# Seven products in another order: splitting A22·T4 a second time and computing (A12 − S2)·R22 last

## The chip, the cores and the metric

The kernel runs on one core of one Trainium2 chip. That core has five engines with instruction queues of their own: TensorE (PE in the profile; its weight loads are listed apart as PEld), VectorE (DVE), ScalarE (ACT), GpSimd (POOL) and SyncE (SP). In this kernel every engine's instructions run in the order in which the program writes them; semaphores hold an instruction back until what it needs is there. The metric is the device time of one execution in microseconds. The kernel before takes 731.65 us, the median of three runs (731.50 to 731.73).

## The reference, cut to what matters

Two branches work on the same x of 2048 rows by 1024 columns (bf16) and are mixed by a gate for each row:

```
g = sigmoid((x * gate_w).sum(-1, keepdims=True))
a = A(x)                       # q, k, v = x @ wqkv; 32 heads; each row looks at itself and
                               # 7 earlier rows, 2 apart; softmax; o @ wo
h = gelu(x @ w_gate) * (x @ w_up)          # 2048 x 3584
b = h @ w_down
return g * a + (1 - g) * b
```

The last step, o·wo and h·w_down together, is one product of 2048 rows, 4608 columns of inputs (3584 of h scaled by 1 − g, 1024 of o, into which g is already worked) and 1024 columns of output. This step is what the change touches.

## The kernel before, in words

Until about 512 us the kernel computes the gate, q, k and v, the attention and the two projections to h. The h and o that come out are stored to memory and loaded back in tiles as they are needed. The rest of the span, about 217 us, is the last product, and the function `down(s)` writes it for one half of the rows: `down(0)` for rows 0 to 1023, `down(1)` (in which `last` is true) for the others.

**First level.** For each half the product is cut into two by two by two blocks and computed with seven products in place of eight (Strassen's method in Winograd's form). A11, A12, A21, A22 are the blocks of the inputs; R11 to R22 those of the two weights; each block holds 18 tiles of 128 × 512 in bf16 (2304 KB). T1 to T4 are sums of R blocks, formed earlier and kept in memory (`t_d`). S = A21 + A22, AD = A11 − A21, and S2 = A22 − AD is written over A21. I number the products:

| product | operands | product | operands |
|---|---|---|---|
| 1 | A11 · R11 | 5 | S · T1 |
| 2 | A12 · R21 | 6 | S2 · T2 |
| 3 | (A12 − S2) · R22 | 7 | AD · T3 |
| 4 | A22 · T4 | | |

The four blocks of the output are 1 + 2; 1 + 6 + 5 + 3; 1 + 6 + 7 + 4 (T4 carries the sign); and 1 + 6 + 5 + 7. Two buffers in fp32 hold partial sums: `u2` holds product 1, then 1 + 6, then 1 + 6 + 7; `qs` holds product 5, then 1 + 6 + 5.

**A whole product** (`mm`, line 1049) is 72 matmuls of 128 × 512: four row tiles j, 18 tiles deep. **A split product** (`level2`, matmuls on line 1024) applies the same method a second time: seven sub-products of 18 matmuls of 128 × 256, so 126 in all. The sub-products run in a fixed order: two on untouched quarters of the operands, three on the sums number 0, 1 and 2, one on the left sum 3, one on the right sum 2. VectorE makes the sums: `forms_L` (line 985) and `forms_R` (line 993) have four instructions each, and the third of `forms_R` changes a quarter of the operand in place. ScalarE copies partial results from one part of PSUM to another between the sub-products (line 1029): after the first sub-product each of its two results is copied on, and the second sub-product adds onto the very place that is copied. Two more VectorE instructions (`joins`, line 1013) add the part that was kept aside, one after the sixth sub-product, one after the seventh.

**Banks.** The eight PSUM banks are dealt into two sets of four, XT (seen as XP) and VT (seen as VP). A split product adds onto what is in its banks, so ScalarE first zeroes the left halves of the set (`zero_left`, line 1005, two instructions for a set). The right halves are begun by ScalarE's copies.

**What sets the order.** `manual_schedule` takes each engine's instructions in program order. Ahead of `down` a small planner deals VectorE's background work into slots by a priority and a wake time; `run_last` finishes what is left of it, among it the scaling by 1 − g of blocks of half 0 (`scale_task`, line 906; pieces of four tiles). Inside `down` the order is written by hand: `take(rest, k)` issues k VectorE instructions from a prepared list, `run` all that are left. Sums over whole blocks are `comb_task` (line 913; five pieces). Results leave by `add_out` (line 1058, then a store on line 1054, which GpSimd's queue issues, or SyncE's for the last four). Loads (`loads`, lines 814, 816, 829, 832) go out on SyncE's queue in program order. Ten buffers of 18 KB in each partition hold blocks and sums; `plan` says for each half which name lies in which buffer, and a load into a buffer waits until its former content has been read.

**Before, half 0:** product 1 whole, 2 whole, 5 split (VT), 6 split (XT), 3 whole onto product 5 in VT, 7 split (XT), 4 whole (VT). **Half 1** is the same, with product 1 split too. In `down(0)` the sums for product 1 of half 1 are made after the sums for product 7. The step A12 − S2 lies ahead of product 6's right sums in half 0 (three of its five pieces), behind them in half 1. `mid6` is what is issued within product 6: joins of product 5, four ScalarE copies of it into `qs`, the loads of R22, T3 and T4.

The functions that the diff touches, and those that call them:

Of the kernel before, what the change touches and what calls it, by code (L numbers as in the profile page):

```python
# [9 lines left out]
ALU = mybir.AluOpType  # L10
# [5 lines left out]
P = 128  # L16
SC = 512
# [51 lines left out]
def kernel(  # L69
# [12 lines left out]
    nc = tc.nc  # L82
    Bsz, S, D = A_x.shape
# [51 lines left out]
    with tc.manual_schedule(engines={mybir.EngineType.PE, mybir.EngineType.DVE, mybir.EngineType.Activation,  # L135
# [296 lines left out]
        def bg(gen, prio, wake):  # L432
            t = Task(gen, prio, wake)
            tasks.append(t)
            tasks.sort(key=lambda t_: t_.prio)
            return t
# [437 lines left out]
        def tf_close():  # L874
            while tf_q[0] < N1:
# [5 lines left out]
        at_end(TFE - 1, tf_close)  # L881

        plan = [dict(A11=4, R11=5, A12=2, R21=7, A21=6, A22=3, T1=1, T2=9, S=8, AD=0, L5=4, R5=5, L6=7, R6=1,
                     R22=4, T3=8, T4=5, L7=7, R7=1),
                dict(A11=6, R11=9, L1=2, R1=4, A12=0, R21=7, A21=8, A22=1, T1=5, T2=4, S=6, AD=3, L5=9, R5=2, L6=7, R6=5,
                     R22=9, T3=6, T4=2, L7=7, R7=5)]
        u2 = regf(R_U2, 4 * SC).rearrange("p (j n) -> p j n", j=4)
        qs = regf(R_QS, 4 * SC).rearrange("p (j n) -> p j n", j=4)
        on = [0]
# [8 lines left out]
        def Bs(s):  # L898
            return {k: bufs[v] for k, v in plan[s].items()}

        def scale_task(b, s, c, ia, ib):
            t0 = s * SUP + c * SC
            om = omgrep[:, t0:t0 + SC].rearrange("p (o s) -> p o s", o=1)
            for i0 in range(ia, ib, 4):
                i1 = min(i0 + 4, ib)
                TT(out=b[:, i0:i1, :], in0=b[:, i0:i1, :], in1=om.to_broadcast([P, i1 - i0, SC]), op=ALU.mult)
                yield 0.05 + 0.273 * (i1 - i0)

        def comb_task(o_, a, b, op, step=4):
            for i0 in range(0, NK, step):  # L910
                i1 = min(NK, i0 + step)
                f = lambda t_: flat(t_[:, i0:i1, :])
                TT(out=f(o_), in0=f(a), in1=f(b), op=op)  # L913
                yield 0.05 + 0.273 * (i1 - i0)

        def run(*gens):
            for g in gens:
                for _ in g:
                    pass

        def pieces(*gens):
            for g in gens:
                yield from g

        def take(g, k):
            for _ in range(k):
                if next(g, None) is None:
                    break
# [14 lines left out]
        def pre_down_2(s):  # L943
            pd["end"] = True
            load_A(Bs(s)["A22"], s, 1, 1, 0, NE_, False)
            for k, c in (("A12", 0), ("A22", 1)):
                bg(scale_task(Bs(s)[k], s, c, 0, NE_), 7, n)
            if now[0] >= NX0 + 3:
                pre_down_3(s)

# [37 lines left out]
        def forms_R(f, b):  # L988
            f = quads(f)
            q = lambda kh, h: quarter(b, kh, h)  # L990
            for o_, a, b_, op in ((f[:, 0], q(0, 1), q(0, 0), ALU.subtract), (f[:, 1], q(1, 1), f[:, 0], ALU.subtract),
                                  (q(0, 1), q(1, 1), q(0, 1), ALU.subtract), (f[:, 2], q(1, 0), f[:, 1], ALU.subtract)):
                TT(out=o_, in0=a, in1=b_, op=op)  # L993
                yield 1.3

        def woven(*gens):
            for cs in zip(*gens):
                yield from cs
# [12 lines left out]
        def joins(bk, rf):  # L1011
            for i in range(2):
                TT(out=two_banks(bk, i, 1), in0=two_banks(bk, i, 1), in1=part5(rf), op=ALU.add)  # L1013
# [26 lines left out]
        def down(s):  # L1040
            B = Bs(s)
            last = s == 1
            eng = nc.gpsimd
            base = s * SUP
            XT, VT = (6, 7, 0, 1), (2, 3, 4, 5)

            def mm(ps, L, R, j, start, q0=0, q1=NK):
                for q, i in list(enumerate(KORD))[q0:q1]:
                    nc.tensor.matmul(ps, lhsT=L[:, i, j * P:(j + 1) * P], rhs=R[:, i, :], start=(start and q == 0),  # L1049
                                     stop=(q == NK - 1), skip_group_check=not start)  # L1050

            def emit(ot, c, nh, j):
                r0 = base + c * SC + j * P
                (nc.sync if last and (c, nh) == (1, 0) else eng).dma_start(out=o2[r0:r0 + P, nh * SC:(nh + 1) * SC], in_=ot)  # L1054

            def add_out(ps, t_, c, nh, j):
                ot = out_tile()
                TT(out=ot, in0=ps, in1=t_, op=ALU.add)  # L1058
                emit(ot, c, nh, j)

            A11, A12, A21, A22, S, AD = (B[k] for k in ("A11", "A12", "A21", "A22", "S", "AD"))
            XP = [bank(XT[j]) for j in range(4)]
            VP = [bank(VT[j]) for j in range(4)]
            if last:
                run(scale_task(A12, s, 0, 0, NE_))
                level2(XT, A11, B["R11"], B["L1"], B["R1"])
                rest = comb_task(AD, A11, A21, ALU.subtract)
                run(scale_task(A21, s, 1, 0, NE_))
                take(rest, 3)
                joins(XT, B["R1"])  # L1070
                for j in range(4):
                    nc.scalar.copy(out=u2[:, j, :], in_=XP[j])
                run(rest)
                loads(s, "T2")
            else:
                for j in range(4):
                    mm(XP[j], A11, B["R11"], j, True, 0, NK - 2)
                    if j == 0:
                        yield
                for j in range(4):  # L1080
                    mm(XP[j], A11, B["R11"], j, True, NK - 2, NK)
                    nc.scalar.copy(out=u2[:, j, :], in_=XP[j])
                run(scale_task(A21, s, 1, KX, NE_), comb_task(S, A21, A22, ALU.add), comb_task(AD, A11, A21, ALU.subtract))
            zero_left(VT)
            if last:
                run(scale_task(A22, s, 1, 0, NE_), comb_task(S, A21, A22, ALU.add))
            for j in range(4):
                mm(XP[j], A12, B["R21"], j, False)
                ot = out_tile()
                nc.scalar.copy(out=ot, in_=XP[j])  # L1090
                emit(ot, 0, 0, j)
            zero_left(XT)
            run(woven(forms_L(B["L5"], S), forms_R(B["R5"], B["T1"])))
            run(comb_task(A21, A22, AD, ALU.subtract))
            S2 = A21
            level2(VT, S, B["T1"], B["L5"], B["R5"])
            run(forms_L(B["L6"], S2))
            rest = comb_task(A12, A12, S2, ALU.subtract)
            if not last:
                take(rest, 3)  # L1100
            run(forms_R(B["R6"], B["T2"]), rest)

            def mid6():
                joins(VT, B["R5"])
                for j in range(4):
                    nc.scalar.copy(out=qs[:, j, :], in_=VP[j])  # L1106
                loads(s, "R22", "T3", "T4")

            level2(XT, S2, B["T2"], B["L6"], B["R6"], mid6)
            if not last:  # L1110
                loads(1, "A11", "R11")
            joins(XT, B["R6"])
            for j in range(4):
                TT(out=u2[:, j, :], in0=XP[j], in1=u2[:, j, :], op=ALU.add)
                TT(out=qs[:, j, :], in0=qs[:, j, :], in1=u2[:, j, :], op=ALU.add)
            zero_left(XT)
            rest = woven(forms_L(B["L7"], AD), forms_R(B["R7"], B["T3"]))
            for j in range(4):
                mm(VP[j], A12, B["R22"], j, False)
                take(rest, 2)  # L1120
                add_out(VP[j], u2[:, j, :], 0, 1, j)
            run(rest)
            if not last:
                N = Bs(1)
                run(scale_task(N["A11"], 1, 0, 0, NE_))
                run(woven(forms_L(N["L1"], N["A11"]), forms_R(N["R1"], N["R11"])))
            level2(XT, AD, B["T3"], B["L7"], B["R7"])
            joins(XT, B["R7"])
            if not last:
                loads(1, "A12", "A21", "R21", "A22")  # L1130
            for j in range(4):
                add_out(XP[j], qs[:, j, :], 1, 1, j)
                TT(out=u2[:, j, :], in0=XP[j], in1=u2[:, j, :], op=ALU.add)
            if not last:
                zero_left(XT)
            for j in range(4):
                mm(VP[j], A22, B["T4"], j, True)
                add_out(VP[j], u2[:, j, :], 1, 0, j)
            if not last:
                loads(1, "T1")  # L1140

        n = len(units)
# [78 lines left out]
```

## Time and profile before

| | |
|---|---|
| median of three runs | 731.65 us |
| the profiled execution | 731.21 us |
| its span | 729.4 us |
| last end of a matmul | 725.96 us |
| matmuls of half 0 in `down`, first to the start of half 1 | 512.48 to 623.39 us |
| matmuls of half 1 | 623.39 to 725.96 us |
| busy over the span: TensorE, VectorE, ScalarE, GpSimd | 714.7, 655.1, 317.2, 114.7 us |

The times in the profile are microseconds from the span's start. A line of the timeline gives the start, the length, the engine, the line of the kernel, the operation, what it writes and reads, how many instructions are merged in it and, in brackets, how long the engine was idle before it and who ended that. TensorE's busy time counts matmuls whose ends are modelled. The start of one group and the start of the next are therefore the better measure of what a product takes.

### The profile page before, as it was taken

Reading aid. Unit: us, or ns where it says so; the run is one execution under the profiler, and the core shown is the slowest. Engines: PE = TensorE matmul, PEld = TensorE weight load, DVE = VectorE, ACT = ScalarE, POOL = GpSimd, SP = SyncE. Lnnn points to the kernel's source line nnn. Section 1 sums busy time; section 2 is a strip of 40 time slices with the busy share of each in tenths; the row PEclk is TensorE's granted clock in tenths of the full one; section 3 lists DMA queues with packets and bytes.
Section 4 is the critical chain, followed back from the end, with each engine's and each line's share of the span. In section 5 each row is a group of like instructions: output and inputs, shape, how many; then the busy total and the mean of one; then the engine's idle time right before and its main releaser. Section 6 shows DMA issues by size and latency. Waiting matters only on the chain. (4 is left out here: it accounts for less than half of the span.)

```text
span 729.4 us, 10330 instructions
## 1 busy us (share of the span) xinstructions
PE 714.7 (98%) x3883; PEld 393.0 (54%) x3945; DVE 655.1 (90%) x703; ACT 317.2 (43%) x570; POOL 114.7 (16%) x212
## 2 busy tenths in 40 slices
PE   8999999999999999999999999999998999999998
PEld 4466666655544444444444444444457666758573
DVE  3699999999999999999999999999599698799944
ACT  4554445444557665555555555555131211232210
POOL 1233445143201210000010000001110011110001
PEclk9999999999999999999999999999999899999999
DMA  9967644287274834443363836563975766965501
GB/s 279 279 184 224 206 140 154 78 283 268 98 213 136 284 118 146 137 154 113 120 203 115 276 118 224 133 234 100 364 315 179 271 229 211 380 276 199 199 22 58
DMA packets 112626, 140.78 MB, mean 193 GB/s; under 512 B 18832, under 2 KB 94768, under 8 KB 111552
## 3 DMA queue, kind: packets, MB, share of 16 engines
q1 hardware_dynamic: 98368, 98.38, 42.0%
q0 software_dynamic: 13920, 41.21, 15.7%
q8 instruction: 31, 0.51, 0.3%
q10 hardware_dynamic: 288, 0.52, 0.3%
q14 instruction: 19, 0.16, 0.1%
HBM read 98.01 MB, written 39.99 MB: 189 GB/s over the span
## 5 line engine op out<-in xcount | busy, mean ns | idle before, releaser
L364 PE MATMUL banks<-arena 128*128 128x512 bf16 x2136 | 472.1, 380 | 4.1 <-DVE arena L401 0.7
L364 PEld LDWEIGHTS <-arena 128*128 128x128 bf16 x2184 | 240.2, 111 | 235.6 <-issue 7.0
L1049 PE MATMUL banks<-arena 128*128 128x512 bf16 x492 | 109.3, 379 | 1.0 <-ACT arena L1106 0.4
L401 DVE TENSOR_TENSOR arena<-banks,arena 128x1024 bf16<-128x1024 f32 x78 | 95.2, 1220 | 13.0 <-PE banks L364 7.6
L1024 PE MATMUL banks<-arena 128*128 128x256 bf16 x882 | 100.3, 277 | 3.7 <-DVE arena L993 3.7
L387 ACT COPY arena<-banks 128x512 f32<-128x512 f32 x78 | 45.7, 586 | 130.8 <-PE banks L364 130.8
L1024 PEld LDWEIGHTS <-arena 128*128 128x128 bf16 x882 | 87.3, 99 | 16.8 <-issue 4.2
L1049 PEld LDWEIGHTS <-arena 128*128 128x128 bf16 x504 | 49.2, 98 | 59.1 <-issue 0.6
L372 ACT CAST arena<-banks 128x512 bf16<-128x512 f32 x102 | 59.6, 584 | 42.4 <-PE banks L364 42.4
L743 DVE TENSOR_TENSOR arena<-arena 128x2048 bf16<-128x2048 bf16 x64 | 77.0, 1219 | 0.5
L750 DVE TENSOR_TENSOR arena<-arena 128x2048 bf16<-128x2048 bf16 (+2 forms) x96 | 73.8, 775 | 1.0
L596 DVE TENSOR_TENSOR arena<-arena 128x2048 bf16<-128x2048 bf16 x64 | 74.6, 1218 | 0.1
L394 ACT COPY banks<-banks 128x512 f32<-128x512 f32 x78 | 44.5, 570 | 21.9 <-PE banks L364 20.1
L258 POOL DMA_DIRECT2D h_d<-arena x28 | 15.1, 541 | 242.0 <-DVE arena L252 213.1
L382 ACT COPY banks<-banks 128x512 f32<-128x512 f32 x78 | 45.0, 576 | 13.6 <-PE banks L364 12.1
L1054 POOL DMA_DIRECT2D out_dram<-arena x28 | 15.2, 541 | 179.8 <-DVE arena L1058 130.0
L913 DVE TENSOR_TENSOR arena<-arena 128x2048 bf16<-128x2048 bf16 (+1 forms) x40 | 41.9, 1110 | 0.0
L1029 ACT COPY banks<-banks 128x256 f32<-128x256 f32 x42 | 14.9, 356 | 57.2 <-PE banks L1024 57.0
L321 DVE TENSOR_TENSOR arena<-arena 128x1024 bf16<-128x1024 bf16 x60 | 38.6, 685 | 0.5
L252 DVE TENSOR_TENSOR arena<-arena 128x2048 bf16<-128x2048 bf16 x28 | 34.0, 1216 | 5.5 <-ACT arena L372 4.1
L370 ACT ACTIVATE arena<-banks 128x512 bf16<-128x512 f32 x54 | 32.2, 597 | 15.4 <-PE banks L364 15.4
L985 DVE TENSOR_TENSOR arena<-arena 128x2304 bf16<-128x2304 bf16 x28 | 37.5, 1352 | 0.5
(85 smaller groups left out, 434.1 us busy)
## 6 DMA issues: line engine op xcount, KB each, us to landing
arena<-t_d SPq DMA_DIRECT2D x8, 2304.0 KB, 12.5
h_d<-arena POOLq DMA_DIRECT2D x28, 512.0 KB, 3.6
arena<-in_B_w_down_dram SPq DMA_DIRECT2D x6, 1792.0 KB, 14.5
t_d<-arena POOLq DMA_DIRECT2D x36, 256.0 KB, 4.1
arena<-h_d SPq DMA_DIRECT2D x6, 1536.0 KB, 11.0
arena<-in_B_w_gate_dram SPq DMA_DIRECT2D x15, 512.0 KB, 5.2
arena<-in_B_w_up_dram SPq DMA_DIRECT2D x15, 512.0 KB, 4.6
arena<-in_B_w_down_dram SPq DMA_DIRECT2D x28, 256.0 KB, 7.0
```

Of the source, the lines that this page charges most:

```text
L364: self.pe = nc.tensor.matmul(ps, lhsT=self.L[form](kt), rhs=rhs[:, kt, :], start=(start and kt == 0), stop=(kt == HK - 1), skip_group_chec ...
L372: nc.scalar.copy(out=o_, in_=i_)
L382: nc.scalar.copy(out=self.Y, in_=self.X)
L387: nc.scalar.copy(out=self.p5s, in_=self.V)
L394: nc.scalar.copy(out=self.Z, in_=self.Y)
L401: TT(out=self.T[:, :, c2s], in0=pair, in1=self.p5s.rearrange("p (o n) -> p o n", o=1).to_broadcast([P, 2, SC]), op=ALU.add)
L596: TT(out=dst, in0=q.rearrange("p (o s) -> p o s", o=1).to_broadcast([P, NWIN, AC]), in1=_win_ap(k, [[-DIL, NWIN], [1, AC]]), op=ALU.mult)
L743: TT(out=prod2[(t // 2) % 2][:, t % 2], in0=ab, in1=_win_ap(v[:, t, HALO:HALO + AC], [[SJ, NJ], [-DIL, NWIN], [1, SJ]]), op=ALU.mult)
L750: TT(out=out_, in0=h(0), in1=h(1), op=ALU.add)
L913: TT(out=f(o_), in0=f(a), in1=f(b), op=op)
L1024: nc.tensor.matmul(c(i, h, j), lhsT=l[:, kt, j * P:(j + 1) * P], rhs=r[:, kt, :], start=False, stop=(kt == KH - 1), skip_group_check=True)
L1049: nc.tensor.matmul(ps, lhsT=L[:, i, j * P:(j + 1) * P], rhs=R[:, i, :], start=(start and q == 0), stop=(q == NK - 1), skip_group_check=not ...
```

## The change

Product 4 is split as well, in both halves, so that a half has one whole product fewer. Product 3 stays whole, but moves to the end of the half, into VT afresh, and no longer onto product 5; its block of the output comes from `qs` and no longer from `u2`. The sequence of a half is now 1, 2, 5, 6, 7 (in VT), 4 (in XT), 3 (in VT).

Around it: the joins of product 5 come ahead of the third right sum of product 6, and A12 − S2 behind all of product 6's sums in both halves. `mid6` zeroes VT for product 7 and loads T3 alone. T4 and R22 are loaded after product 6. Four of product 7's eight sums are issued ahead of the joins of product 6 and the additions into `u2`, four behind; then the additions into `qs`, then `zero_left(XT)` for product 4, then product 7. The loads of A11 and R11 for half 1 are issued after product 7 and no longer after product 6. In half 0 the scaling of A11 and the eight sums for product 1 of half 1 are dealt among the row tiles of product 3. The last stores, now those of product 3, go on SyncE's queue in half 1. In the work that is left over before `down(0)`, A22 is scaled ahead of the last piece of A12. The buffers are dealt anew.

```
-                     R22=4, T3=8, T4=5, L7=7, R7=1),
-                dict(A11=6, R11=9, L1=2, R1=4, A12=0, R21=7, A21=8, A22=1, T1=5, T2=4, S=6, AD=3, L5=9, R5=2, L6=7, R6=5,
-                     R22=9, T3=6, T4=2, L7=7, R7=5)]
+                     T3=8, L7=4, R7=5, T4=9, L4=1, R4=7, R22=6),
+                dict(A11=0, R11=4, L1=5, R1=8, A12=3, A21=9, R21=1, A22=7, T1=2, AD=6, S=0, T2=8, L5=4, R5=5, L6=1, R6=2,
+                     T3=0, L7=4, R7=5, T4=8, L4=2, R4=1, R22=9)]
...
-            for k, c in (("A12", 0), ("A22", 1)):
-                bg(scale_task(Bs(s)[k], s, c, 0, NE_), 7, n)
+            for k, c, ia, ib in (("A12", 0, 0, 8), ("A22", 1, 0, NE_), ("A12", 0, 8, NE_)):
+                bg(scale_task(Bs(s)[k], s, c, ia, ib), 7, n)
...
-                (nc.sync if last and (c, nh) == (1, 0) else eng).dma_start(out=o2[r0:r0 + P, nh * SC:(nh + 1) * SC], in_=ot)
+                (nc.sync if last and (c, nh) == (0, 1) else eng).dma_start(out=o2[r0:r0 + P, nh * SC:(nh + 1) * SC], in_=ot)
...
             run(forms_L(B["L6"], S2))
-            rest = comb_task(A12, A12, S2, ALU.subtract)
-            if not last:
-                take(rest, 3)
-            run(forms_R(B["R6"], B["T2"]), rest)
+            rest = forms_R(B["R6"], B["T2"])
+            take(rest, 2)
+            joins(VT, B["R5"])
+            run(rest, comb_task(A12, A12, S2, ALU.subtract))
 
             def mid6():
-                joins(VT, B["R5"])
                 for j in range(4):
                     nc.scalar.copy(out=qs[:, j, :], in_=VP[j])
-                loads(s, "R22", "T3", "T4")
+                zero_left(VT)
+                loads(s, "T3")
 
             level2(XT, S2, B["T2"], B["L6"], B["R6"], mid6)
-            if not last:
-                loads(1, "A11", "R11")
+            loads(s, "T4", "R22")
+            rest = woven(forms_L(B["L7"], AD), forms_R(B["R7"], B["T3"]))
+            take(rest, 4)
             joins(XT, B["R6"])
             for j in range(4):
                 TT(out=u2[:, j, :], in0=XP[j], in1=u2[:, j, :], op=ALU.add)
+            run(rest)
+            for j in range(4):
                 TT(out=qs[:, j, :], in0=qs[:, j, :], in1=u2[:, j, :], op=ALU.add)
             zero_left(XT)
-            rest = woven(forms_L(B["L7"], AD), forms_R(B["R7"], B["T3"]))
+            level2(VT, AD, B["T3"], B["L7"], B["R7"])
+            if not last:
+                loads(1, "A11", "R11")
+            run(woven(forms_L(B["L4"], A22), forms_R(B["R4"], B["T4"])))
+            joins(VT, B["R7"])
             for j in range(4):
-                mm(VP[j], A12, B["R22"], j, False)
-                take(rest, 2)
-                add_out(VP[j], u2[:, j, :], 0, 1, j)
-            run(rest)
-            if not last:
-                N = Bs(1)
-                run(scale_task(N["A11"], 1, 0, 0, NE_))
-                run(woven(forms_L(N["L1"], N["A11"]), forms_R(N["R1"], N["R11"])))
-            level2(XT, AD, B["T3"], B["L7"], B["R7"])
-            joins(XT, B["R7"])
+                add_out(VP[j], qs[:, j, :], 1, 1, j)
+                TT(out=u2[:, j, :], in0=VP[j], in1=u2[:, j, :], op=ALU.add)
+            level2(XT, A22, B["T4"], B["L4"], B["R4"])
+            joins(XT, B["R4"])
+            for j in range(4):
+                add_out(XP[j], u2[:, j, :], 1, 0, j)
             if not last:
                 loads(1, "A12", "A21", "R21", "A22")
+                zero_left(XT)
+                N = Bs(1)
+                rest = pieces(scale_task(N["A11"], 1, 0, 0, NE_), woven(forms_L(N["L1"], N["A11"]), forms_R(N["R1"], N["R11"])))
             for j in range(4):
-                add_out(XP[j], qs[:, j, :], 1, 1, j)
-                TT(out=u2[:, j, :], in0=XP[j], in1=u2[:, j, :], op=ALU.add)
+                mm(VP[j], A12, B["R22"], j, True)
+                if not last:
+                    take(rest, 3)
+                add_out(VP[j], qs[:, j, :], 0, 1, j)
             if not last:
-                zero_left(XT)
-            for j in range(4):
-                mm(VP[j], A22, B["T4"], j, True)
-                add_out(VP[j], u2[:, j, :], 1, 0, j)
-            if not last:
+                run(rest)
                 loads(1, "T1")
```

## The prediction

> **What bounds the kernel now.** I read the page first, then the table of the last product by stretches, the chain that ended last, and the timeline of half 0 around the places that the diff names.
>
> ```profile
> PE 714.7 (98%) x3883; PEld 393.0 (54%) x3945; DVE 655.1 (90%) x703; ACT 317.2 (43%) x570; POOL 114.7 (16%) x212
> ```
>
> TensorE is the bound over the whole span, and VectorE is close behind. So fewer matmuls help only where VectorE follows. The stretches of the last product (from:to, length, busy time and count of each engine, granted clock, DMA share, GB/s):
>
> ```profile
> 562.40:566.10 3.70, 0.03 (x2) 0.01 (x1) 3.63 (x4) 0.00 (x0) 0.00 (x0) 0.81 1.16 444
> 566.10:571.50 5.40, 5.40 (x26) 3.74 (x26) 5.36 (x5) 0.74 (x2) 0.00 (x0) 0.50 0.51 218
> 571.50:578.60 7.10, 7.10 (x67) 6.31 (x66) 2.18 (x4) 3.40 (x8) 0.00 (x0) 1.00 0.70 246
> 652.70:680.90 28.20, 27.86 (x253) 24.59 (x252) 27.90 (x26) 7.88 (x21) 0.54 (x1) 1.00 0.48 173
> ```
>
> The first two rows show TensorE stopped and then at half its clock for 5.4 us: the stop costs more than its own length. In the last row VectorE and TensorE are both full, so half 1 has no room for more VectorE work there. The chain agrees; it runs through VectorE's sums until product 3 of half 1 starts, and through TensorE from there to the end:
>
> ```profile
> 674.52 4.14 DVE arena L913 x4
> 679.67 0.62 DVE banks L1013
> 681.38 10.74 PE banks L1049 x49
> 696.65 13.75 PE banks L1024 x126
> ```
>
> In the timeline of half 0 two things matter: the wait in product 6, and when ScalarE's zeroing gets through.
>
> ```profile
> 566.08 12.64 PE L1024 MATMUL banks<-arena 128*128 128x256 bf16 x90 [3.67 <-DVE arena L993]
> ...
> 578.56 15.70 PE L1049 MATMUL banks<-arena 128*128 128x512 bf16 x70
> ...
> 581.60 0.60 ACT L1005 ACTIVATE banks<-omgrep 128x512 f32<-128x512 bf16 x1 [4.38 <-DVE arena L1114]
> ...
> 584.41 0.60 ACT L1005 ACTIVATE banks<-omgrep 128x512 f32<-128x512 bf16 x1 [2.21 <-DVE arena L1114]
> ...
> 594.10 13.92 PE L1024 MATMUL banks<-arena 128*128 128x256 bf16 x126
> ...
> 595.34 0.36 ACT L1029 COPY banks<-banks 128x256 f32<-128x256 f32 x1 [10.32 <-PE banks L1024]
> ```
>
> The zeroing (line 1005) waits for the additions into `u2` (line 1114), and ScalarE's next copy (line 1029) comes behind it. Today a whole product, which needs nothing of ScalarE, runs meanwhile, so this costs nothing.
>
> **Prices, all from this trace.** A whole product 15.5 us (578.56 to 594.10). A split product 13.75 (594.10 to 607.85), so one sub-product 1.965. A sum for a split product 1.27 (eight from 540.54 to 550.69). A scaling piece 1.14 (six in 6.8, from 624.20). A block sum of five pieces 5.2 to 5.3. Two joins 1.3. An addition out of PSUM 0.6. A ScalarE zeroing 0.6, a copy 0.36.
>
> **The change, part by part.**
>
> *Product 4 split:* 15.5 − 13.75 = 1.8 us of TensorE saved in each half. VectorE gets eight sums and two joins, 10.15 + 1.3 = 11.5 us in each half; whether they are hidden follows below.
>
> *A12 − S2 behind product 6's sums:* three pieces, 3.4 us, leave the way of product 6's right sums. The wait of 3.67 goes, and with it the half clock: 90 matmuls took 12.64 where 90 × 13.75 / 126 = 9.8 is their due, so 2.8. Together 6.5 us, in half 0 only. Next late would be the right sum 0, which I put below 3 us ahead of need.
>
> *A22 scaled ahead of A12's last piece:* VectorE waited 3.00 us for that piece (until 525.37), while A22's load, issued at 504.6 and 11.7 us under way, was there. Three pieces fill the wait, so VectorE runs 3.0 us earlier and starts the sums for product 5 at 537.5 (before, 540.54). T1 bounds it: its load landed 19.0 us after 518.5, at 537.5. The gain lies between 0 and 3.0; I take 3.0 because that load is needed by the second sum only.
>
> *Product 7 straight behind product 6:* here the change adds a wait. ScalarE's order is now: the zeroing of XT, then product 7's copies. The zeroing waits for `u2`, `u2` for the joins of product 6, and these for product 6's end. Product 7's second sub-product adds onto what the copy must first read, so TensorE can issue one sub-product and then stops. Even an idle VectorE leaves 1.3 + 2.45 + 1.2 + 0.4 = 5.3 us after product 6 against 1.965 of work. And VectorE isn't idle; half 0, in us from the span's start:
>
> VectorE: 537.5 + 10.15 (sums 5) + 5.3 (S2) + 5.1 (left sums 6) + 2.55 (two right sums) = 560.6, the right sum 0 being ready at 559.4; + 1.3 (joins) + 2.55 + 5.2 (A12 − S2) + 5.1 (four sums for 7) = 574.8; + 1.3 (joins of 6) + 2.45 (`u2`) = 578.5. TensorE: product 5 ends at 544.42 + 13.75 = 558.2, product 6 needs that right sum at 562.1 and ends at 572.0, one sub-product of product 7 ends at 573.95. Zeroing and copy let the second start at 579.7: a wait of 5.7. It is longer than the 3.67 that halved the clock, so I add that row's 2.8. The bounds are 0 and 3.4, half of the 6.8 us from the fall of the clock (a mean of 0.81 over 3.7 us means that its last 1.4 ran at half, so 564.7) to its return at 571.5. Product 7 ends at 579.7 + 11.8 + 2.8 = 594.3, product 4 at 608.05, product 3 at 623.6. Product 4's sums are done by 597, its third pair before need. Half 1 thus starts at 623.6, where it did (623.39): +0.2.
>
> [...]
>
> *Half 1, a chain of VectorE.* Its work from product 4's joins on (second join from 608.3 to 608.95): stores' additions 2.4, scaling A11 3.4, sums for product 1 10.15, product 3's additions 2.4, scaling A12 and A21 6.8, AD 5.2, joins 1.3, scaling A22 3.4, S 5.3, sums 5 10.15, S2 5.3, left sums 6 5.1, right sums 6 5.1, joins 1.3, A12 − S2 5.2, four sums 5.1, joins 1.3, `u2` 2.45: together 81.35, so 690.3. Nothing makes it wait: product 3's row tiles end at 611.9, 615.8, 619.7, 623.6, each before its addition is due. On the way the joins of product 1 start at 637.5 (three pieces of AD are ahead), while that product ends at 637.35; product 2 starts 1.4 us after the joins start (679.59 to 680.95 is that step before), at 638.9: a wait of 1.5. Products 2, 5 and 6 end at 654.4 and, with 27.9 for the pair as in 652.69 to 680.57, at 682.3. Product 7's first sub-product ends at 684.25, the zeroing and the copy at 691.5: a wait of 7.2, and 2.8 for the clock. Product 7 ends at 691.5 + 11.8 + 2.8 = 706.1, product 4 at 719.85, product 3 at 735.4. Before it was 725.96: +9.4 us.
>
> *Loads, queues, stores, at nothing each.* A11 and R11 of half 1 go out at 594.3 instead of 578.10; the longest landing of these kinds is 17.5 us, to 611.8, and A11 is scaled from 611.4, R11 used from 617: up to 0.4. The next four go out at 608.05 (607.39 before) and are used 2.7 us later than before. T3, issued at 558.5 without R22 ahead, lands 8.8 to 12.5 us later, by 571.0; its first use is at 572. T4, issued after product 6 at 572.0, lands by 584.5; its sum comes at 587.5. On SyncE's queue nothing else waits behind these. The number of stores is unchanged on each queue, and the tail from the last matmul to the span's end stays 3.44. If a load's cover is gone, VectorE's chain takes the excess one to one.
>
> **The sum.** Half 0: −1.8 − 6.5 + 5.7 + 2.8 = +0.2. Half 1: −1.8 − 0.4 (wait ahead of product 3 today) + 1.5 + 7.2 + 2.8 = +9.3. Together +9.5, by the chain +9.4. The profiled execution of 731.21 (span 729.4) becomes 740.6; the median is 0.44 above it, so 741.0.
>
> **Rivals.**
>
> *No hold on ScalarE (faster):* product 7's copies go through before the zeroing, or don't need it. Against it stands that the zeroing came before the copies in the trace, in program order. The point: the second zeroing must be over by 573.95, and it can't be before 576.9. Then product 7 waits only for its third pair of sums (1.2 in half 0). Half 0 ends at 616.3, `u2` in half 1 at 686.05, and TensorE at 688.6 + 5.9 + 13.75 + 15.5 = 723.8. That is −2.1: 729.5.
>
> *The hold without the clock:* both waits stay, the clock doesn't fall: 741.0 − 5.6 = 735.4. Against it: both are longer than the 3.67 that halved it.
>
> *VectorE doesn't get its 3 us, or a load or a finer wait holds it up by as much:* all of half 0's chain and with it half 1's shift: 744.0. For it: T1 lands on the very start of the sums. With 3.4 twice for the clock it would be 745.2.
>
> **How the numbers follow.** Two executions of this kernel differ by up to 0.23 us; 0.2%, 1.5 us, is what a measurement can tell from no change. The forecast (741, own range 738 to 743) has 0.70, VectorE later 0.15, the clock staying up 0.07, no hold 0.05, and 0.03 for a partial hold that ends within 0.2%. The range goes from 735.4 to 745.2. Faster 0.05, same 0.03, slower 0.92.
>
> **What would show it.** Right: zeroings of XT that wait for the additions into `u2` and stand just ahead of product 7's first copies; TensorE idle about 5.7 and 7.2 us inside product 7 with a ScalarE copy as releaser; the clock at 0.50 behind both; no wait in product 6 of half 0; half 1 starting at about 623.6; 1134 matmuls of 128 × 256 in the two halves. Wrong: no idle TensorE inside product 7, or a wait that VectorE's sums end. The step likeliest to be off is half 1's chain of 81 us on VectorE, in which 0.02 us an instruction already makes 1.4 us.

## The result, and the profile after

The changed kernel takes 742.94 us (median of four runs, 741.74 to 743.35) against 731.69 for the kernel before, measured beside it: a ratio of 1.0149, with a 95% interval from 1.0132 to 1.0167. It is 1.5% slower. The forecast was 741.0 with a range from 735.4 to 745.2. The profiled execution took 743.35 us, its span 741.6.

The page's line of engines (busy us, share of the span, instructions):

```profile
PE 719.0 (97%) x4053; PEld 406.4 (55%) x4053; DVE 676.6 (91%) x723; ACT 324.8 (44%) x590; POOL 115.1 (16%) x212
```

VectorE has 21.5 us more to do, near the 23 that the two splits add. TensorE is the bound in name only: it waits more than before (15.4 us in three stops, where before had 3.67 and 0.39), and part of its busy time is at half clock. The last product by stretches (from:to, length, busy time and count of PE, PEld, DVE, ACT, POOL, then granted clock, DMA share, GB/s):

```profile
574.70:582.20 7.50, 0.12 (x2) 0.05 (x1) 7.50 (x10) 1.57 (x4) 0.00 (x0) 0.86 1.02 384
582.20:587.50 5.30, 5.30 (x28) 3.77 (x28) 5.30 (x7) 0.17 (x1) 0.00 (x0) 0.55 0.58 183
...
639.30:641.90 2.60, 0.16 (x2) 0.00 (x0) 2.60 (x5) 0.61 (x2) 0.00 (x0) 0.93 1.13 429
641.90:645.00 3.10, 3.07 (x8) 1.12 (x8) 3.10 (x4) 2.46 (x5) 0.00 (x0) 0.51 1.02 433
...
688.70:694.30 5.60, 0.06 (x2) 0.03 (x1) 5.60 (x8) 1.55 (x4) 0.00 (x0) 0.86 0.98 390
694.30:700.00 5.70, 5.70 (x29) 4.00 (x29) 5.70 (x7) 0.20 (x1) 0.00 (x0) 0.54 0.88 280
```

Three stops of TensorE, each followed by a stretch at about half clock: in product 7 of half 0, ahead of product 2 of half 1, in product 7 of half 1. VectorE is busy through all of them. The timeline at the first stop shows what ends it:

```profile
577.47 1.29 DVE L1013 TENSOR_TENSOR banks<-banks,arena 128x512 f32<-128x512 f32 x2
578.67 2.47 DVE L1115 TENSOR_TENSOR arena<-banks,arena 128x512 f32<-128x512 f32 x4
580.03 0.60 ACT L1005 ACTIVATE banks<-omgrep 128x512 f32<-128x512 bf16 x1 [7.72 <-DVE arena L1115]
...
581.23 0.60 ACT L1005 ACTIVATE banks<-omgrep 128x512 f32<-128x512 bf16 x1 [0.59 <-DVE arena L1115]
581.77 0.60 ACT L1029 COPY banks<-banks 128x256 f32<-128x256 f32 x2
582.15 28.02 PE L1024 MATMUL banks<-arena 128*128 128x256 bf16 x234 [7.38 <-ACT banks L1029]
```

Joins (1013), additions into `u2` (1115), the zeroing of XT (1005), product 7's copies (1029), TensorE: each starts when the one before ends. ScalarE was idle 7.72 us with the copies next in its queue. In the kernel before, the same zeroing waited 4.38 and 2.21 us for the same additions, and nothing came of it. The waits of the other two stops:

```profile
641.93 17.17 PE L1049 MATMUL banks<-arena 128*128 128x512 bf16 x72 [2.47 <-ACT arena L1072]
...
694.27 28.27 PE L1024 MATMUL banks<-arena 128*128 128x256 bf16 x234 [5.54 <-ACT banks L1029]
```

**Where the time came from.** From the start of product 5 of half 0 to VectorE's addition right behind the last matmul it was 181.6 us (544.42 to 725.98) and is now 193.1 (544.98 to 738.12): +11.6. The stretch before that took 0.56 us longer in this execution: the last product itself began at 513.03 instead of 512.48 us, and over the twelve traces of this document that start scatters from 512.48 to 513.71. I take what the half clock costs from the start of a group to the start of the next, less its due at full clock:

| term | us |
|---|---|
| two products split, 2 × 1.8 | −3.6 |
| product 6 of half 0: no wait (3.67), no half clock (12.48 − 9.82) | −6.3 |
| the wait ahead of product 3 in half 1 | −0.4 |
| waits 7.38 + 2.47 + 5.54 | +15.4 |
| half clock behind them: 27.85 − 25.54, 17.01 − 15.54, 28.11 − 25.54 | +6.4 |
| sum | +11.5 |

### The profile page after: what moved, and what is told of

It is laid out like the page before. It is cut to its first block, busy times and chain, and to the rows that moved or that the text cites. A ratio compares the mean times of both kernels' runs of the same rounds, so it can differ in the third digit from the quotient of the medians.

```text
span 741.6 us, 10660 instructions
## 1 busy us (share of the span) xinstructions
PE 719.0 (97%) x4053; PEld 406.4 (55%) x4053; DVE 676.6 (91%) x723; ACT 324.8 (44%) x590; POOL 115.1 (16%) x212
## 5 line engine op out<-in xcount | busy, mean ns | idle before, releaser
L364 PE MATMUL banks<-arena 128*128 128x512 bf16 x2184 | 474.8, 379 | 1.5 <-DVE arena L401 0.7
L364 PEld LDWEIGHTS <-arena 128*128 128x128 bf16 x2184 | 240.5, 111 | 235.2 <-issue 7.0
L1024 PE MATMUL banks<-arena 128*128 128x256 bf16 x1134 | 129.8, 279 | 12.9 <-ACT banks L1029 12.9
L1024 PEld LDWEIGHTS <-arena 128*128 128x128 bf16 x1134 | 113.2, 100 | 29.6 <-issue 13.6
L1049 PE MATMUL banks<-arena 128*128 128x512 bf16 x360 | 80.0, 384 | 2.5 <-ACT arena L1072 2.5
L1049 PEld LDWEIGHTS <-arena 128*128 128x128 bf16 x360 | 35.6, 99 | 45.6 <-issue 4.6
L985 DVE TENSOR_TENSOR arena<-arena 128x2304 bf16<-128x2304 bf16 x36 | 48.2, 1349 | 0.4
L993 DVE TENSOR_TENSOR arena<-arena 128x2304 bf16<-128x2304 bf16 x36 | 48.4, 1348 | 0.2
L1029 ACT COPY banks<-banks 128x256 f32<-128x256 f32 x54 | 19.0, 355 | 56.1 <-PE banks L1024 55.9
## 6 DMA issues: line engine op xcount, KB each, us to landing
arena<-h_d SPq DMA_DIRECT2D x6, 1536.0 KB, 11.5
```

The source lines that it names most:

```text
L364: self.pe = nc.tensor.matmul(ps, lhsT=self.L[form](kt), rhs=rhs[:, kt, :], start=(start and kt == 0), stop=(kt == HK - 1), skip_group_chec ...
L1024: nc.tensor.matmul(c(i, h, j), lhsT=l[:, kt, j * P:(j + 1) * P], rhs=r[:, kt, :], start=False, stop=(kt == KH - 1), skip_group_check=True)
```

## The experiments

The kernel before ran beside each, at medians from 732.2 to 732.6. Runs made at different times are compared by their ratios to it. The theory: ScalarE's order (zeroing of XT, then copies) holds product 7. The rivals: VectorE's work as a whole is the bound, whatever ScalarE does; and, for the half clock, that it costs nothing beyond the wait.

**1. The zeroing moved behind the copies, nothing else.**

```
-            zero_left(XT)
-            level2(VT, AD, B["T3"], B["L7"], B["R7"])
+            level2(VT, AD, B["T3"], B["L7"], B["R7"], lambda: zero_left(XT))
```

> The changed kernel with one move: the zeroing of XT is issued within product 7, behind its ScalarE copies, and no longer ahead of product 7. My theory (ScalarE's order holds product 7): TensorE no longer stops behind the first sub-product; it waits only for the third pair of sums, about 3.3 us in half 0 and 2.7 in half 1, and the waits of 7.38 and 5.54 in the changed kernel go. Working the chain again with these gives 734 us (732 to 736). Rival (VectorE with its 23 us more is the bound, wherever ScalarE zeroes): the same VectorE work in the same order, so no change within 0.3%, 741 to 744 us.

Measured 732.87 us, ratio 1.0010 (1.0000 to 1.0019). One ScalarE instruction pair, moved behind five sub-products, is worth 1.4% or 10.2 us. The waits of its TensorE:

```profile
583.42 21.49 PE L1024 MATMUL banks<-arena 128*128 128x256 bf16 x180 [3.24 <-DVE arena L993]
604.75 15.70 PE L1049 MATMUL banks<-arena 128*128 128x512 bf16 x70
...
638.19 17.39 PE L1049 MATMUL banks<-arena 128*128 128x512 bf16 x70 [3.98 <-ACT arena L1072]
...
692.12 19.82 PE L1024 MATMUL banks<-arena 128*128 128x256 bf16 x180 [1.02 <-DVE arena L993]
```

ScalarE's copies hold nothing any more; VectorE's third pair of sums does (line 993), 3.24 us as expected and 1.02 where I had 2.7. Ahead of product 2 of half 1 the wait grew from 2.47 to 3.98. Counted from the start of product 5 of half 0, TensorE begins half 1 4.8 us sooner than in the changed kernel and product 2 only 3.3 us sooner, for VectorE's joins of product 1 come forward by 3.25 us only, counted in the same way (they start at 636.83 and 640.57). So the hold explains nearly all of the loss, and without it the change brings nothing.

**2. The joins and `u2` ahead of all eight sums.** In the changed kernel `take(rest, 4)` ahead of `joins(XT, B["R6"])` is left out.

> The changed kernel, its zeroing where it was, but the joins of product 6 and the additions into u2 come ahead of all eight sums for product 7 and not behind four. My theory: the hold stays but shrinks to what is left even for a VectorE that is free: joins, additions, zeroing and copy after product 6, about 2.6 us of wait inside product 7 in each half, too short or nearly so for the clock; about 733.6 us. If the hold were due to VectorE's sums being late and not to the zeroing, the sums, now 3.8 us later, would make it worse: 745 us or more.

Measured 735.63, ratio 1.0045 (1.0030 to 1.0060). The direction is the theory's: with the sums later the time fell by 1.0%. The hold inside product 7 shrank to what the chain behind product 6 needs by itself:

```profile
577.71 27.37 PE L1024 MATMUL banks<-arena 128*128 128x256 bf16 x234 [2.27 <-ACT banks L1029]
...
639.15 0.59 PE L1049 MATMUL banks<-arena 128*128 128x512 bf16 x1 [4.77 <-ACT arena L1072]
```

The size was 2 us off: I had the clock at full behind so short a wait, though the changed kernel's trace had it at 0.51 behind 2.47, and 27.21 − 25.54 = 1.7 us went there; and product 2 of half 1 waits 4.77.

**3. More work for TensorE behind the hold.** `fill` is 60 in half 0 and 46 in half 1, for product 7 alone.

```
+            for i in range(fill):
+                nc.tensor.matmul(c(0, 1, 0), lhsT=lq(0, 0)[:, i % KH, 0:P], rhs=rq(0, 0)[:, i % KH, :], start=False,
+                                 stop=(i == fill - 1), skip_group_check=True)
             prod(0, 0, lq(0, 1), rq(1, 0))
```

> The changed kernel with idle work for TensorE in the place of the wait: 60 (half 0) and 46 (half 1) extra matmuls of 128 x 256 behind product 7's first sub-product, 6.5 and 5.0 us at full clock, into a part of the banks that a ScalarE copy overwrites later. They use the time in which TensorE waits, and keep it busy. If the half clock behind the waits costs what I took (2.5 and 2.7 us in the changed kernel's trace), the time falls by about 5 us to 738 (737 to 739), with the clock at 1.00 behind product 7's second sub-product. If VectorE's chain absorbs it, or the clock falls whatever TensorE does, it stays at 742 to 744.

Measured 754.72, ratio 1.0308 (1.0293 to 1.0323). The experiment missed its aim: the extra matmuls waited themselves.

```profile
582.13 8.71 PE L1032 MATMUL banks<-arena 128*128 128x256 bf16 x60 [7.52 <-ACT banks L1029]
590.68 21.56 PE L1024 MATMUL banks<-arena 128*128 128x256 bf16 x196
```

They write the other half of the bank that the copy reads; whether they would have waited in another bank no run shows. They ran behind the hold, and the run tells something else: 106 matmuls of 0.109 us, 11.6 us, moved the ratio from 1.0149 to 1.0308: 1.59% of 731.7, again 11.6 us. What TensorE does behind the hold lies on the path nearly in full, in both halves: in the traces, counted from product 5 of half 0, half 1 starts 6.4 us later and product 3 of half 1 11.2 us later.

**4. The same matmuls ahead of product 7's first sub-product.**

> The same extra matmuls (60 in half 0, 46 in half 1), now ahead of product 7's first sub-product, so that they can run in the time in which TensorE waits and not behind it; the wait left should be about 0.8 and 0.5 us. My theory: the half clock behind the two waits cost 2.5 and 2.7 us; with TensorE busy the clock stays at 1.00 and the time falls from 742.9 to about 738 (737 to 739.5), although TensorE does 11.5 us more. Rival (the clock's loss is absorbed by VectorE's chain): half 0's loss is absorbed, half 1's alone is saved, 740; or (the clock falls at any wait) nothing is saved, 743.

Measured 740.11, ratio 1.0107 (1.0081 to 1.0132): 0.42% or 3.1 us less than the changed kernel (the two intervals just touch), although TensorE does 11.6 us more. Half 0 went as meant: 0.83 us of wait left, clock 1.00 behind it, 2.3 us saved there. In half 1 it didn't:

```profile
582.57 25.71 PE L1024 MATMUL banks<-arena 128*128 128x256 bf16 x234 [0.83 <-ACT banks L1029]
...
640.83 15.70 PE L1052 MATMUL banks<-arena 128*128 128x512 bf16 x72 [3.26 <-ACT arena L1075]
...
693.18 27.37 PE L1024 MATMUL banks<-arena 128*128 128x256 bf16 x234 [2.01 <-ACT banks L1029]
```

Product 7 of half 1 started early, the 46 matmuls were over too soon, a wait of 2.01 was left, and 27.21 − 25.54 = 1.7 us went to the half clock again (a mean of 0.64 from 693.2 to 698 us). So a part of the clock's loss reaches the end; 3.1 us of my 5 are shown. The first rival's 740 came out, but not its mechanism: the 2.3 us of half 0 were not absorbed there, as half 1 starts 78.26 us after product 5 of half 0 and no longer 80.56.

**5. 62 instead of 46 in half 1.**

> As the run with 60 and 46 extra matmuls ahead of product 7, but with 62 in half 1. There a wait of 2.01 us was left in half 1 and 1.8 us were lost to the half clock behind it. My theory (the clock's loss in half 1 lies on the path in full): the wait left is about 0.3, the loss goes, and the time falls by 1.8 to 738.3 us (737.3 to 739.3). Rival (the loss is absorbed, product 4 or 3 waits for VectorE instead): 740 as before.

Measured 741.78, ratio 1.0125 (1.0110 to 1.0140). Product 7 has no half clock in either half (1.00 in both), yet nothing is gained over run 4: neither the theory's 738.3 nor the rival's 740. This time the wait ahead of product 2 in half 1 (3.42) was followed by a half clock (0.50 from 642 to 646 us), for 18.39 − 0.22 − 15.54 = 2.6 us, where in run 4 a wait of 3.26 was not (1.00 behind it). Product 7 of half 1 then started 2.5 us later, at 686.51 (684.02 in run 4). Its extra matmuls reached beyond the hold, about 2.4 us too far. The zeroing was over at 692.49 and a copy takes 0.36, so without them the second sub-product could have started at about 692.9. With them the first one started at 693.28 and took 1.97, so the second came at about 695.2. That uses up what the half clock had cost there, 1.7 us in run 4 and 2.6 in the changed kernel. How much of the clock's 6.4 us would come back with all three stops filled stays open.

**6. The scaling order of before.** `(("A12", 0, 0, NE_), ("A22", 1, 0, NE_))` in the changed kernel.

> The changed kernel, with A12 scaled whole ahead of A22 as before. I had forecast 3.0 us for this step; the changed kernel's trace shows that VectorE still waited twice for loads (0.93 each) and started the block sums about 1.0 us earlier, not 3.0, relative to TensorE. Theory now: the step is worth 0.5 to 1.5 us, so 743.5 to 744.5 without it. If it were worth the 3.0 after all: 746.

Measured 744.28, ratio 1.0166 (1.0140 to 1.0192). The two intervals overlap, so the time alone doesn't settle it; the holds in its trace were 8.00 and 7.03 instead of 7.38 and 5.54, which is the direction of a small gain. In the changed kernel VectorE waited again, for the next loads:

```profile
527.26 1.23 DVE L906 TENSOR_TENSOR arena<-arena,omgrep 128x2048 bf16<-128x2048 bf16 x1 [0.93 <-DMA arena<-h_d]
...
529.41 0.42 DVE L906 TENSOR_TENSOR arena<-arena,omgrep 128x512 bf16<-128x512 bf16 x1 [0.93 <-DMA arena<-h_d]
```

A better measure is VectorE's lead, from its first sum for product 5 to TensorE's start of that product. It is 1.90, 3.13 and 3.88 us in the three traces with the old order (runs 9 and 6, and the kernel before) and 4.75 to 5.13 in the nine with the new one. With the old order VectorE waited 4.98, 3.75 and 3.00 us for A12's last tile. So the step is worth about 1 to 3 us of lead, by when that load lands, and the kernel before, from whose trace I forecast, was the one in which it landed soonest.

**7. Product 4 whole in the new order.** No sums for it, no joins, no zeroing ahead of product 7.

```
-            zero_left(XT)
...
-            run(woven(forms_L(B["L4"], A22), forms_R(B["R4"], B["T4"])))
...
-            level2(XT, A22, B["T4"], B["L4"], B["R4"])
-            joins(XT, B["R4"])
             for j in range(4):
+                mm(XP[j], A22, B["T4"], j, True)
                 add_out(XP[j], u2[:, j, :], 1, 0, j)
```

> The changed kernel's order, with product 4 whole in XT: no second split, so no sums for it, no joins and no zeroing of XT ahead of product 7 (the hold has no cause left). TensorE has 3.6 us more than with the split, VectorE 23 us less. Theory (the split costs VectorE more than TensorE gains, even without the hold): product 7 of half 0 still waits for its third pair of sums (about 3.3 and 1.8 for the clock), the wait ahead of product 2 of half 1 (3.98 and 1.7 for the clock with the zeroing moved) goes: about 729 us, less than the 732.9 of the split version with the zeroing moved. Rival (the split is a gain once the hold is gone): 732.9 + 3.6 = 736.5.

Measured 734.98, ratio 1.0038 (1.0021 to 1.0056). My theory (729) fell, and the rival (736.5) was nearer: the split is worth 0.28%, 2 us of the 3.6, once the hold is gone. The trace shows my mistake:

```profile
583.55 7.73 PE L1024 MATMUL banks<-arena 128*128 128x256 bf16 x54 [3.03 <-DVE arena L993]
...
690.94 7.41 PE L1024 MATMUL banks<-arena 128*128 128x256 bf16 x54 [3.68 <-DVE arena L993]
```

I had the wait for the third pair of sums in half 0 alone. It comes in both halves even with 11.5 us less for VectorE in each, since the block sum A12 − S2, joins and `u2` stand ahead of those sums, and product 7 now follows product 6 at once. (Run 8 puts all eight sums ahead of the joins and `u2`, and the wait in product 7 is gone.) These waits and their half clock are 3.03 + 3.68 + 1.7 + 1.3 = 9.7 us: a price of the order, not of the split.

**8. All eight sums ahead, zeroing moved.** Run 1 with `run(rest)` in the place of `take(rest, 4)`.

> The changed kernel with the zeroing of XT moved into product 7, and all eight sums of product 7 ahead of the joins of product 6 and the additions into u2. With the zeroing moved alone, product 7 waited 3.24 and 1.02 us for its third pair of sums, with 1.8 for the clock in half 0, and product 2 of half 1 waited 3.98 with 1.7 for the clock. Theory (what is left is VectorE's work as a whole, which ran nearly without a gap from 553 to 716 us): the waits in product 7 go, but half 1 starts no earlier for VectorE, so the wait ahead of product 2 grows to 6 or 7; the time falls by 1 to 2 us only, to 731 to 732. Rival (the waits are separate and each is a matter of order): 6 us less, 727.

Measured 732.45, ratio 1.0006 (0.9993 to 1.0018). The theory's outcome, a little above its range: product 7 has no wait, and nearly all of it comes back, 1.3 us in three short waits of product 4 of half 0 and the rest ahead of product 2 of half 1.

```profile
638.77 0.58 PE L1049 MATMUL banks<-arena 128*128 128x512 bf16 x1 [7.67 <-ACT arena L1072]
```

Line 1072 is the copy of product 1 into `u2`, behind joins that VectorE reaches only now. Without the hold, VectorE bounds the changed kernel up to product 2 of half 1; from there TensorE runs to the end without a wait. But not all of that is work: on this way VectorE stood 3.4 us for stores of results, 2.93 and 0.43 (1.10 and 0.96 in run 1).

```profile
609.52 0.69 DVE L1058 TENSOR_TENSOR arena<-banks,arena 128x512 bf16<-128x512 f32 x1 [2.93 <-DMA out_dram<-arena]
```

Whether more room for results waiting to be stored would bring these back no run shows.

**9. One part of the change on the kernel before.** A12 − S2 behind product 6's right sums in half 0.

```
             rest = comb_task(A12, A12, S2, ALU.subtract)
-            if not last:
-                take(rest, 3)
             run(forms_R(B["R6"], B["T2"]), rest)
```

> The kernel before with one part of the change: in half 0 the three pieces of A12 - S2 come behind product 6's right sums. My theory: the wait of 3.67 us in product 6 and the 2.8 us of half clock behind it go, and nothing takes their place, since VectorE has about 10 us of idle time later in half 0: 731.65 - 6 = 725.6 us (724.5 to 727). Rival (half 1 is bound by VectorE, which starts it no earlier): the gain is lost by product 2 or 5 of half 1, 730 to 732.

Measured 728.22, ratio 0.9945 (0.9930 to 0.9959): faster, by 4 us and not by 6. A wait stayed in product 6, as the right sums still came behind all four left ones and VectorE was 2 us later in this execution. It had waited 4.98 us for A12's last tile, 3.00 in the trace of before:

```profile
527.53 4.97 DVE L906 TENSOR_TENSOR arena<-arena,omgrep 128x2048 bf16<-128x2048 bf16 x5 [4.98 <-DMA arena<-h_d]
...
564.84 11.62 PE L1024 MATMUL banks<-arena 128*128 128x256 bf16 x90 [2.24 <-DVE arena L993]
```

**10. The same, with the sums of product 6 dealt alternately and A22 scaled ahead.** The scaling is the change's line. In the place of the lines that made product 6's sums and A12 − S2 stands:

```
+            run(woven(forms_L(B["L6"], S2), forms_R(B["R6"], B["T2"])), comb_task(A12, A12, S2, ALU.subtract))
```

> The kernel before with A12 - S2 behind product 6's sums, as in the second experiment on that kernel, and two more edits: left and right sums for product 6 dealt alternately, and A22 scaled ahead of the last piece of A12 (a part of the change). With A12 - S2 late alone a wait of 2.24 us stayed in product 6, with 1.8 for the clock, as the right sums came behind all four left ones. Theory: both go and nothing waits in their place, 728.2 - 4 = 724 to 725.5 us. Rival: product 3, which in that order follows product 6 at once, now waits for A12 - S2 (up to 2.8 us and the clock), 727 to 730.

Measured 724.83 (724.61 to 725.03), ratio 0.9897 (0.9877 to 0.9918). This is the fastest version, 1.0% ahead of the kernel before and 2.5% ahead of the changed one, with no product more split. TensorE goes through without a wait, at a granted clock of 1.00 all the way:

```profile
544.93 27.83 PE L1024 MATMUL banks<-arena 128*128 128x256 bf16 x252
572.60 15.70 PE L1049 MATMUL banks<-arena 128*128 128x512 bf16 x72
588.14 13.92 PE L1024 MATMUL banks<-arena 128*128 128x256 bf16 x126
601.89 15.70 PE L1049 MATMUL banks<-arena 128*128 128x512 bf16 x72
```

The two further edits were made together, so which of them took away the wait isn't shown. VectorE's lead is 5.03 us here and was 1.90 in run 9, and that difference alone is more than the wait of 2.24; dealing the sums alternately may have added nothing.

This kernel splits the same products as run 7 and is 1.4%, 10.3 us, faster than it; run 7's waits and half clock in product 7 were 9.7.

## Why the prediction was right, point by point

**The hold of product 7 by ScalarE's order:** right in place, sequence and releaser. Run 1 takes it away by itself, and 10.2 of the 11.3 us go. Its sizes were 5.7 and 7.2 us forecast against 7.38 and 5.54. The misses, +1.7 and −1.7, cancel in the sum. In part that follows from the mechanism: in half 1 VectorE's chain ends the hold, so what TensorE loses ahead of it only shortens it. TensorE came to the stop at 688.73 instead of 684.25, because half 1 began at 625.54 instead of 623.6 and product 2 lost 2.4 us more than forecast, while `u2` was done at 693.26 instead of 690.3. That the two misses are equal is luck.

**A22 scaled ahead of A12's last piece, 3.0 us:** too large, and the reason for the 7.38. I had looked up that A22's load was there, and not that the loads behind it, A12's last tile and A21's, come later still: VectorE waited twice for 0.93. Measured from VectorE's first sum for product 5 to TensorE's start of that product, the lead grew from 3.88 us (540.54 to 544.42) to 4.93 (540.05 to 544.98): 1.05. My bounds were 0 and 3.0, and I took the end. Run 6 shows that the size moves with the load: the step is worth about 1 to 3 us, and least against the trace that I read. The rival in which VectorE doesn't get its 3 us (744.0) thus came true for two of the three.

**Product 6's wait and its half clock gone, 6.5 us:** right. Product 6 of half 0 has no wait in the changed kernel, and run 9 shows that most of this gain is to be had without the rest of the change.

**Half 1's chain on VectorE, 81.35 us from product 4's joins to `u2`:** near. In the trace it runs from 610.97 (the end of the second join) to 693.26, 82.3 us, of which 1.05 is a wait for a store of results, which I had not seen. I said that nothing makes it wait, although the trace of before has such a wait too, 2.57 us ahead of 619.86.

**The wait ahead of product 2 of half 1, 1.5 us:** 2.47. I gave it no loss to the clock; it had 1.5.

**The clock, 2.8 for each hold:** 2.3 and 2.6. (The row of before, from start to start as above, gives 2.7.) That row stands behind a wait of 3.67; a shorter one halved the clock too: here a wait of 2.47 sufficed, with a clock of 0.51 behind it.

**The sum:** waits 14.4 forecast and 15.4 measured, clock 5.6 and 6.4, and 0.56 in the stretch before product 5 of half 0, which lies within the scatter of the start. The profiled span came out at 741.6 instead of 738.8.

**The rivals:** no hold (729.5) did not happen, and run 1 shows that it would not have been faster either: 732.87, since product 2 of half 1 then waits 3.98 with 1.7 for the clock, which I had not carried into that sum, and the wait for the third pair in half 0 is 3.24 with 1.7 for the clock where that sum has 1.2. The hold without the clock (735.4) did not happen either: the clock fell behind all three stops.

## What to carry to other kernels

Here a zeroing that waited held up what stood behind it in its own queue: ScalarE was idle 7.72 us ahead of it, with the copies next, and TensorE waited 7.38. Before moving work, ask of each engine's queue what comes next and whether the new neighbour is needed sooner; a cheap zeroing placed one product too early cost 1.4% here. Before saving matmuls by more element-wise sums, ask whether the engine that makes the sums has time: here the second split was worth 2 us of its 3.6 even without the hold. The change held a real gain, three VectorE instructions behind a chain instead of in it, and that part was worth 4 us when it was made alone.

## What the runs showed of the hardware that I had not expected

The half clock followed much shorter stops than I had thought, one of 2.01 us among them, but not each time: behind 2.58 and 3.26 nothing was lost. What is lost is, where the rows show it, time that TensorE works at a granted clock of about a half, 0.50 to 0.55. Over the traces of before, after and the ten runs, TensorE's waits of 1 us and more in the last product, and what was lost behind each, start to start less the due (us; down the columns):

| wait | lost | wait | lost | wait | lost | wait | lost |
|---|---|---|---|---|---|---|---|
| 1.02 | 0.0 | 2.47 | 1.5 | 3.42 | 2.6 | 5.54 | 2.6 |
| 1.02 | 0.0 | 2.58 | 0.0 | 3.67 | 2.7 | 7.03 | 2.1 |
| 2.01 | 1.7 | 3.03 | 1.7 | 3.68 | 1.3 | 7.38 | 2.3 |
| 2.23 | 0.4 | 3.14 | 2.6 | 3.98 | 1.7 | 7.52 | 2.0 |
| 2.24 | 1.6 | 3.24 | 1.7 | 4.22 | 1.7 | 7.67 | 2.2 |
| 2.27 | 1.7 | 3.26 | 0.0 | 4.77 | 1.8 | 8.00 | 1.6 |

The two waits of 1.02 lost nothing. Of the ten between 2 and 3.3 two lost nothing and one 0.4. The twelve longer ones lost 1.3 to 2.7 each, with little regard to their length. The same kernel can go either way: of the 17 executions of the kernel before beside runs 4, 6, 7 and 10, two with a mean granted clock of 1.000 took 728.9 and 729.1 us, the other fifteen, at 0.994 to 0.997, 731.0 to 734.2. Run 9's four were two at 727.4 (0.999 and 1.000) and two at 729.0 and 729.2 (0.998), and its trace, one of the latter, lost 1.6 behind its wait. What the runs don't show is the cause of this scatter.
